# One decode step with a sliding key/value window on one core: how 512 output rows and two small inputs are loaded

## The chip, the cores and the metric

The kernel runs on one core of one Trainium2 chip. A core has four compute engines that run side by side, each with its own instruction stream: TensorE (PE, matrix products; its weight loads are listed as PEld), VectorE (DVE), ScalarE (ACT) and GpSimd (POOL). A fifth, SyncE (SP), here only issues transfers. Transfers between the main memory (HBM) and the on-chip memory (SBUF, 128 partitions) are carried out by 16 DMA engines, whoever issues them. The metric is the device time of one execution, in microseconds (us); lower is better.

## The reference

```python
xn = layernorm(x)                                   # x: 1 x 1 x 512
# A: attention over the last W = 4096 of 32768 cached positions, 32 heads of 128
q = xn @ wq                                         # 512 x 4096
p = softmax(q . k[window] / sqrt(128))              # per head
o = p @ v[window]
s = o.reshape(4096) @ wo                            # 4096 x 512
# B: a gated block of the same xn (for one token the shifted groups are all zero)
h  = gelu(layernorm(xn) @ w1); hs = shift(h) @ w2
x1 = xn + hs
g  = silu(x1 + gelu(layernorm(x1) @ w3) @ w4)       # w3: 512 x 1376
out = x + s * g
```

Everything is bfloat16. The window of K and of V is 32 heads x 4096 positions x 128, 33.5 MB each; wq and wo have 4.2 MB each, w2, w3 and w4 together 3.3 MB. Each element is used once or twice, so nearly all of the work is bringing it in.

## The kernel before

Loads go through one helper, which issues them from SP, in program order:

```python
def load(dst, src):
    return tc.keep_in_program_order(nc.sync.dma_start(out=dst, in_=src))

x_bf = small.tile([P, KC], BF16, name="x_bf")
nc.scalar.dma_start(out=x_bf[:], in_=A_x.rearrange("a b (p c) -> p (a b c)", p=P))
x_row = small.tile([P, P], BF16, name="x_row")
nc.gpsimd.memset(x_row[:], 0.0)
nc.scalar.dma_start(out=x_row[0:P:32, :], in_=A_x.rearrange("a b (j n) -> (a b j) n", j=KC))
w2_sb = ...; load(w2_sb[:], ...)                     # 512 KB
w3_sb = ...; load(w3_sb[:], ...)                     # 1376 KB
...                                                  # w4 in three parts, wq (4096 KB)
```

The layer norm of x, the block B and q come first. In the layer norm GpSimd computes the power -1/2:

```python
nc.gpsimd.tensor_tensor(out=rstd[:], in0=rstd[:], in1=neg_half[:], op=ALU.pow)
```

Then come 16 pairs of heads. K of a pair is one load of 2 MB over 128 partitions (six buffers), V another (three buffers, which take the space of the weights once q is there). DVE computes half of the scores of a pair (a product, line 302, and a sum, line 304), PE the other half through transposes; PE multiplies V:

```python
for s in range(NP + LAG):                            # NP = 16 pairs, LAG = 3
    h = s - LAG
    kn = load_kv(k_pool, A_k_cache, s) if s < NP else None
    if s == LAG:
        wts_guard.__exit__(None, None, None)         # the weights' space becomes V's
        v_pool = ctx.enter_context(tc.tile_pool(name="v", bufs=V_BUFS))
        wo_blk[few_block] = v_pool.tile([64, 8, D], BF16, tag="wo_few", bufs=1, name="wo_few")
        wo_rows = v_pool.tile([P, H - h_part, D], BF16, tag="wo_rows", bufs=1, name="wo_rows")
    if last:
        v = load_kv(v_pool, A_v_cache, h, cuts)      # the last V in three pieces
    elif h >= 0:
        v = load_kv(v_pool, A_v_cache, h)
    if h in (7, 12):
        load_wo(h // 12)
    if h == 4:
        load_few()
    if last:
        load_rows(H - 2, 2)
    ...
```

The output rows wo come in parts. Heads 0 to 15 and 16 to 23 are two blocks of 128 partitions (load_wo). Heads 28 to 31 (h_part = H - 4) are loaded row by row into wo_rows: heads 28 and 29 ahead of the last piece of V, heads 30 and 31 after it. Heads 24 to 27 are the part called wo_few, on 64 partitions with 8 rows (8 KB) each, loaded by GpSimd:

```python
def load_few():
    def step(k):
        nc.gpsimd.dma_start(out=scratch[0:k, :],
                            in_=A_x[0, 0, 0:4 * k].rearrange("(p c) -> p c", p=k))
    def part(p0, k):
        nc.gpsimd.dma_start(
            out=wo_blk[few_block][p0:p0 + 8 * k],
            in_=A_wo[few_h * P + 8 * p0:few_h * P + 8 * p0 + 64 * k, :].rearrange(
                "(a b t) n -> a b (t n)", a=k, b=8))
    scratch = small.tile([16, 4], BF16, name="scratch")
    step(15)
    part(0, 6)
    step(2)
    part(48, 2)
    step(7)
```

The step loads bring a few elements of x into a scratch tile that nothing reads[...]. In the built program GpSimd's order is: layer norm's power, step 15, step 2, the second layer norm's power, step 7, and then the two parts. All parts of wo are added into one PSUM tile, y_ps, by matmuls of one column of o (line 151). At the end y_ps is multiplied by g, x is added, and 1 KB is written out.

Of the kernel before, what the change touches and what calls it, by code (L numbers as in the profile page):

```python
# [8 lines left out]
P = 128  # L9
BF16 = mybir.dt.bfloat16  # L10
FP32 = mybir.dt.float32
# [7 lines left out]
G = 4  # L19
LAG = 3  # L20
K_BUFS = 6
V_BUFS = 3
EARLY = 4
LATE = 14
# [4 lines left out]
def kernel(  # L29
# [14 lines left out]
    nc = tc.nc  # L44
# [3 lines left out]
    _, H, Sk, Dh = A_k_cache.shape  # L48
# [6 lines left out]
    KC = D // P  # L55
# [13 lines left out]
    ps_o = ctx.enter_context(tc.tile_pool(name="ps_o", bufs=1, space=PSUM))  # L69
    ps_y = ctx.enter_context(tc.tile_pool(name="ps_y", bufs=1, space=PSUM))  # L70
    sm_pool = ctx.enter_context(tc.tile_pool(name="sm", bufs=3))
    small.tile([P, 128], BF16, name="pad")
    wts_guard = tc.tile_pool(name="wts", bufs=1)
    wts = wts_guard.__enter__()

    def load(dst, src):
        return tc.keep_in_program_order(nc.sync.dma_start(out=dst, in_=src))  # L77

    x_bf = small.tile([P, KC], BF16, name="x_bf")
    nc.scalar.dma_start(out=x_bf[:], in_=A_x.rearrange("a b (p c) -> p (a b c)", p=P))  # L80
    x_row = small.tile([P, P], BF16, name="x_row")
    nc.gpsimd.memset(x_row[:], 0.0)
    nc.scalar.dma_start(out=x_row[0:P:32, :], in_=A_x.rearrange("a b (j n) -> (a b j) n", j=KC))
    w2_sb = wts.tile([P, KC, D], BF16, name="w2_sb")
    load(w2_sb[:], B_w2.rearrange("(p c) n -> p c n", p=P))
    w3_sb = wts.tile([P, KC, F], BF16, name="w3_sb")
    load(w3_sb[:], B_w3.rearrange("(p c) n -> p c n", p=P))
    w4_sb = wts.tile([P, 11, D], BF16, name="w4_sb")
# [6 lines left out]
    def load_kv(pool, cache, i, cuts=None):  # L95
        t = pool.tile([P, CP, Dh], BF16, tag="kv", name="kv")
        src = cache[0, 2 * i:2 * i + 2, W0:, :].rearrange("a (b c) d -> b a (c d)", b=P // 2)
        dst = t[:].rearrange("p c d -> p (c d)")
        cuts = cuts or (0, CP)
        for c0, c1 in zip(cuts, cuts[1:]):  # L100
            load(dst[:, c0 * Dh:c1 * Dh], src[:, :, c0 * Dh:c1 * Dh])
            if len(cuts) > 2 and c1 == cuts[-2]:
                load_rows(H - 4, 2)
        return t

    ident_bf = const.tile([P, P], BF16, name="ident_bf")
# [41 lines left out]
    def rows_add(ps, col, w, last):  # L148
        k = col.shape[0]
        for j in range(KC):  # L150
            nc.tensor.matmul(ps[32 * j:32 * j + 1, :], lhsT=col, rhs=w[0:k, j * P:(j + 1) * P],
                             start=False, stop=last, skip_group_check=True)
# [102 lines left out]

    y_ps = ps_y.tile([P, P], FP32, name="y_ps")
    rows_open(y_ps)  # L260
# [83 lines left out]
    def sm_turn(g):  # L344

        s = st[g]
        mt_ps = ps_misc.tile([2, P], FP32, tag="misc", name="mt_ps")
        nc.tensor.transpose(mt_ps[:], s["m1"][:], ident_f[:])  # L348
        mx = sm_pool.tile([2, 2], FP32, tag="mx", name="mx")
        nc.vector.tensor_reduce(out=mx[:], in_=mt_ps[:].rearrange("r (b a) -> r a b", a=2), axis=AX.X,  # L350
                                op=ALU.max)
        nc.vector.scalar_tensor_tensor(out=md[0:2],  # L352
                                       in0=ident_f[0:2, 0:2].unsqueeze(2).to_broadcast([2, 2, 2]),
                                       scalar=-scale, in1=mx[:].unsqueeze(1).to_broadcast([2, 2, 2]),
                                       op0=ALU.mult, op1=ALU.mult)
# [27 lines left out]
    blocks = [(0, 16), (16, 8), (24, 8)]  # L383
    few_block = 2
    few_h = blocks[few_block][0]
    h_part = H - 4
    o_blk, wo_blk, ox_blk = {}, {}, {}

    def load_wo(i):
# [2 lines left out]
        wo_blk[i] = t[:, 0:n, :]  # L392
        load(wo_blk[i], A_wo[h0 * P:(h0 + n) * P, :].rearrange("(p t) n -> p t n", p=P))

    def load_few():
        def step(k):
            nc.gpsimd.dma_start(out=scratch[0:k, :],
                                in_=A_x[0, 0, 0:4 * k].rearrange("(p c) -> p c", p=k))  # L400

        def part(p0, k):
            nc.gpsimd.dma_start(
                out=wo_blk[few_block][p0:p0 + 8 * k],
                in_=A_wo[few_h * P + 8 * p0:few_h * P + 8 * p0 + 64 * k, :].rearrange(
                    "(a b t) n -> a b (t n)", a=k, b=8))

        scratch = small.tile([16, 4], BF16, name="scratch")
        step(15)
        part(0, 6)  # L410
        step(2)
        part(48, 2)
        step(7)

    def wo_row(h):
        return wo_rows[:, h - h_part, :]
# [1 line left out]
    def load_rows(h, n):  # L418
        load(wo_rows[:, h - h_part:h - h_part + n, :],
             A_wo[h * P:(h + n) * P, :].rearrange("(h p) n -> p h n", p=P))  # L420
# [32 lines left out]
    def v_out(h, n):  # L453
        g, hl = divmod(h, G)
        b = [i for i, (h0, _) in enumerate(blocks) if h >= h0][-1]
        if b not in o_blk:
            o_blk[b] = sm_pool.tile([P, blocks[b][1]], BF16, tag=f"o{b}", bufs=1, name="o")
            if b == few_block:
                nc.gpsimd.memset(o_blk[b][:], 0.0)
        c = h - blocks[b][0]  # L460
        if h >= h_part - 2:
            nc.vector.tensor_tensor(out=o_blk[b][:, c:c + n], in0=st[g]["oT"][:, hl:hl + n],  # L462
                                    in1=st[g]["rden"][:, hl:hl + n], op=ALU.mult)
            return
        for k in range(n):
            nc.scalar.mul(o_blk[b][:, c + k:c + k + 1], st[g]["oT"][:, hl + k:hl + k + 1],  # L466
                          st[g]["rden"][:, hl + k:hl + k + 1])
# [10 lines left out]
    def ox_pick(i):  # L478
# [10 lines left out]
                                    op=ALU.add)  # L489
        ox_blk[i] = ox  # L490


    y_row = small.tile([1, D], FP32, name="y_row")

# [7 lines left out]

    def y_block(i):
        for t in range(8):
            k = wo_blk[i].shape[0]
            rows_add(y_ps, ox_blk[i][0:k, t:t + 1], wo_blk[i][:, t, :], False)

    def y_head(h):
        rows_add(y_ps, o_blk[few_block][:, h - few_h:h - few_h + 1], wo_row(h), h == H - 1)
# [8 lines left out]
    for s in range(NP + LAG):  # L518
        h = s - LAG
        last = h == NP - 1  # L520
        kn = load_kv(k_pool, A_k_cache, s) if s < NP else None
        if s == LAG:
            wts_guard.__exit__(None, None, None)
            v_pool = ctx.enter_context(tc.tile_pool(name="v", bufs=V_BUFS))
            wo_blk[few_block] = v_pool.tile([64, 8, D], BF16, tag="wo_few", bufs=1, name="wo_few")
            wo_rows = v_pool.tile([P, H - h_part, D], BF16, tag="wo_rows", bufs=1, name="wo_rows")
        if last:
            v = load_kv(v_pool, A_v_cache, h, cuts)
        elif h >= 0:
            v = load_kv(v_pool, A_v_cache, h)  # L530
        if h in (7, 12):
            load_wo(h // 12)
        if h == 4:
            load_few()
        if last:
            load_rows(H - 2, 2)

        if s < NP:
            turn = [s // 2 - 1] if s % 2 == 0 and s > 0 else []
            k_open(s)  # L540
            k_vector(s, kn, 0)
            k_turn(s, kn)
            for g in turn:
                sm_turn(g)
            if s % 2 == 1 and s >= 3:
                sm_den((s - 3) // 2)
                sm_rden((s - 3) // 2)
            k_scores(s)
            if s % 2 == 1:
                sm_own(s // 2)  # L550
            for g in turn:
                sm_exp(g)
            if s in (12, 15):
                ox_spread(s // 14)
            if s == 11:
                v_add(3)
                v_out(12, 4)
            k_vector(s, kn, 1)
            if h >= 0:
                v_pair(h, v)  # L560
            if s in (12, 15):
                ox_pick(s // 14)
            if s == 13:
                y_wide(0)
            if s % 2 == 1:
                sm_max(s // 2)
            g = (h - 1) // 2
            if h > 0 and h % 2 == 1 and g not in MOVED:
                v_out(G * g, G)
            if h % 2 == 0 and h > 0 and g in MOVED and g != 3:  # L570
                v_add(g)
                v_out(G * g, G)
            if s == NP - 1:
                v_out(2 * h, 2)
        elif s == NP:

            sm_turn(LG)
            y_block(1)
            sm_exp(LG)
            rows_add(y_ps, one_f, y_row, False)  # L580
            v_pair(h, v)
            v_out(2 * h, 2)
            ox_spread(few_block)
            sm_den(LG)
            sm_rden(LG)
            ox_pick(few_block)
        elif not last:
            y_block(few_block)
            v_pair(h, v)
            v_out(2 * h, 2)  # L590
        else:
            for c0, c1 in zip(cuts, cuts[1:]):
                if c1 == CP:
                    for r in range(h_part, H - 2):
                        y_head(r)
                v_pair(h, v, c0, c1)
            v_out(2 * h, 2)
            for r in range(H - 2, H):
                y_head(r)
# [36 lines left out]
```

## Time and profile before

| | |
|---|---|
| time, median of 3 | 199.63 us (199.37 to 199.74) |
| span of the profiled execution | 197.8 us |
| read from HBM | 78.84 MB, 399 GB/s over the span |
| busy PE, PEld, DVE, ACT, POOL | 133.7, 103.2, 145.0, 78.9, 5.7 us |
| mean granted TensorE clock | 0.734 of full speed |

A row of 40 digits in the profile is the span in 40 equal slices of 4.94 us; a digit is the busy share in tenths, 9 for 90% or more. The row "DMA" is the mean share of the 16 DMA engines that have a packet in flight, and GB/s what they moved in the slice: the first can be full while the second is low. The chain of waits follows the work that ended last back from the end, at each step to what released it. In a group or a wait, "A <- B" says that A waited for B, and L302 is line 302 of the kernel.

### The profile page before, as it was taken

The page shows a single profiled execution, that of the slowest core. Times are in us where ns is not written, and L with a number is a line of the kernel's source. Part 1 is how long each engine was busy: PE and PEld are TensorE (multiplying, and loading weights), DVE is VectorE, ACT ScalarE, POOL GpSimd, SP SyncE. Part 2 cuts the span into 40 slices and gives each one's busy share as a digit, 9 for nine tenths or more (in the row PEclk, how much of TensorE's full clock was granted, in tenths as well). Part 3 has the DMA queues.
Part 4 walks back from the last instruction along what each step waited for, and adds up shares of the span by engine and source line. Part 5 has one row for each costly group of instructions (what it writes and reads, how often), then busy time and mean ns, then how long its engine had stood idle before and what let it go on. Part 6 is the DMA issues. An engine that isn't in the chain of part 4 may idle for free.

```text
span 197.8 us, 4706 instructions
## 1 busy us (share of the span) xinstructions
PE 133.7 (68%) x2099; PEld 103.2 (52%) x2099; DVE 145.0 (73%) x160; ACT 78.9 (40%) x173; POOL 5.7 (3%) x17
## 2 busy tenths in 40 slices
PE   0515976877478499759788862946575797875761
PEld 0415255866468393423788541336474636873660
DVE  1540012999999999999999999639899997792201
ACT  2000302978194391530676450335264308753000
POOL 2302100200000000000000000000000000000000
PEclk9999985696755855966967996698555879585555
DMA  6999999998999999999999999999999999999970
GB/s 200 410 444 451 388 424 421 406 257 335 427 426 437 437 426 421 424 434 427 434 427 431 427 421 427 437 427 434 424 427 431 431 424 431 421 437 424 406 279 6
DMA packets 6932, 79.13 MB, mean 400 GB/s; under 512 B 993, under 2 KB 1601, under 8 KB 2113
## 3 DMA queue, kind: packets, MB, share of 16 engines
q1 hardware_dynamic: 6568, 78.32, 95.0%
q0 software_dynamic: 192, 0.52, 1.0%
q8 instruction: 16, 0.26, 0.5%
q10 hardware_dynamic: 152, 0.00, 0.0%
q14 instruction: 4, 0.02, 0.0%
HBM read 78.84 MB, written 0.00 MB: 399 GB/s over the span
## 4 chain that ended last, share of the span: by engine, by line
DMA 44%; DVE 37%; PE 10%; ACT 2%; SPq 2%; issue 2%; POOL 1%; DVEq 0%
DMA kv<-in_A_k_cache_dram 31%; DVE S L304 22%; DVE prod L302 12%; DMA wo_rows<-in_A_wo_dram 7%; DMA scratch<-in_A_x_dram 4%; DMA x_bf<-in_A_x_dram 2%; ACT kt L318 2%; PE hr_ps L222 2%; PE qT_ps L238 2%; SPq L77 2%; PE oT L442 2%; PE a_ps L211 1%; PE hr_ps L219 1%; DVE m L342 1%; PE oT L449 1%
## 5 line engine op out<-in xcount | busy, mean ns | idle before, releaser
L304 DVE TENSOR_REDUCE S<-prod 128x20 f32<-128x2560 bf16 (+1 forms) x32 | 83.8, 2620 | 1.1
L318 ACT COPY kt<-pt 128x1024 bf16<-128x1024 bf16 x54 | 51.0, 1022 | 26.0 <-PE pt L317 26.0
L302 DVE TENSOR_TENSOR prod<-kv,q_bc 128x2560 bf16<-128x2560 bf16 (+1 forms) x32 | 44.3, 1386 | 8.9 <-DMA kv<-in_A_k_cache_dram 6.3
L317 PE MATMUL pt<-ident_bf,kv 128*128 128x128 bf16 x432 | 40.7, 276 | 10.6 <-DMA kv<-in_A_k_cache_dram 8.9
L317 PEld LDWEIGHTS <-kv 128*128 128x128 bf16 x432 | 37.0, 128 | 13.9 <-DMA kv<-in_A_k_cache_dram 10.4
L442 PE MATMUL oT<-pT,kv 128*128 128x2 bf16 x768 | 22.2, 165 | 3.6 <-DMA kv<-in_A_v_cache_dram 3.6
L323 PE MATMUL sT<-qT_bf,kt 128*128 128x2 bf16 x432 | 17.3, 165 | 10.8 <-ACT kt L318 10.2
L442 PEld LDWEIGHTS <-kv 128*128 128x128 bf16 x768 | 21.2, 102 | 5.0 <-DMA kv<-in_A_v_cache_dram 4.9
L323 PEld LDWEIGHTS <-kt 128*128 128x128 bf16 x432 | 15.8, 101 | 13.4 <-ACT kt L318 12.6
L431 PE MATMUL ov<-kv,pT 128*8 128x512 bf16 x64 | 20.5, 491 | 0.0
L431 PEld LDWEIGHTS <-pT 128*8 128x8 bf16 x64 | 6.4, 104 | 12.8 <-issue 9.4
L360 PE MATMUL mb_ps<-md,par_t 4*128 4x4 f32 x16 | 4.0, 315 | 12.0 <-DVE md L352 12.0
L367 ACT ACTIVATE pT<-S,mb 128x64 bf16<-128x64 f32 x32 | 10.9, 356 | 0.2
L363 ACT COPY mb<-mb_ps 128x4 f32<-128x4 f32 x8 | 1.3, 162 | 22.4 <-PE mb_ps L360 22.4
L360 PEld LDWEIGHTS mb_ps<-md,par_t 4*128 4x128 f32 x16 | 3.4, 264 | 12.6 <-issue 11.3
L462 DVE TENSOR_TENSOR o<-oT,rden 128x2 bf16<-128x2 f32 x3 | 0.5, 160 | 11.8 <-PE oT L442 11.8
L466 ACT ACTIVATE o<-oT,rden 128x1 bf16<-128x1 f32 x26 | 4.7, 264 | 5.7 <-PE oT L449 3.8
L225 DVE COPY hr<-hr_ps 1x512 f32<-1x512 f32 x1 | 0.7, 679 | 8.4 <-PE hr_ps L222 8.4
L214 ACT ACTIVATE a_bf<-a_ps 128x10 bf16<-128x10 f32 x1 | 0.2, 179 | 16.3 <-PE a_ps L211 16.3
L211 PE MATMUL a_ps<-z_bf,w_sb 128*128 128x1 bf16 (+1 forms) x44 | 2.6, 194 | 5.5 <-DVE z_bf L199 5.5
L367 ACT ACTIVATION_READ_ACCUMULATOR pT<-S,mb 128x1 f32 x32 | 6.0, 187 | 0.0
L348 PE MATMUL mt_ps<-ident_f,m 128*2 128x128 f32 x8 | 2.7, 340 | 4.5 <-DVE m L342 4.5
(111 smaller groups left out, 93.7 us busy)
## 6 DMA issues: line engine op xcount, KB each, us to landing
kv<-in_A_k_cache_dram SPq DMA_DIRECT2D x16, 2048.0 KB, 27.5
kv<-in_A_v_cache_dram SPq DMA_DIRECT2D x15, 2048.0 KB, 26.6
wq_sb<-in_A_wq_dram SPq DMA_DIRECT2D x1, 4096.0 KB, 18.6
wo<-in_A_wo_dram SPq DMA_DIRECT2D x1, 2048.0 KB, 27.0
w_sb<-in_B_w_dram SPq DMA_DIRECT2D x1, 1376.0 KB, 6.8
w_sb<-in_B_w_dram SPq DMA_DIRECT2D x1, 1024.0 KB, 8.9
wo<-in_A_wo_dram SPq DMA_DIRECT2D x1, 1024.0 KB
kv<-in_A_v_cache_dram SPq DMA_DIRECT2D x1, 1024.0 KB, 12.5
```

The lines of the kernel that those rows point to most:

```text
L77: return tc.keep_in_program_order(nc.sync.dma_start(out=dst, in_=src))
L211: nc.tensor.matmul(a_ps[0:m, j:j + 1], lhsT=w3_sb[:, c, cols], rhs=z3_bf[:, c:c + 1], start=(c == 0), stop=(c == KC - 1))
L302: nc.vector.tensor_tensor(out=prod[:, 0:m, :], in0=kn[:, rows, :], in1=q_bc[:, s:s + 1, :].to_broadcast([P, m, Dh]), op=ALU.mult)
L304: nc.vector.tensor_reduce(out=st[s // 2]["S"][:, s % 2, rows], in_=prod[:, 0:m, :], axis=AX.X, op=ALU.add)
L317: nc.tensor.transpose(pt[:, i, :], kn[:, n + b + i, :], ident_bf[:])
L318: nc.scalar.copy(out=kts[s][:, b:b + w, :], in_=pt[:, 0:w, :])
L323: nc.tensor.matmul(st[s // 2]["sT"][:, s % 2, c, :], lhsT=kt[:, c, :], rhs=qT_bf[:, 2 * s:2 * s + 2], start=True, stop=True)
L360: nc.tensor.matmul(mb_ps[:], lhsT=par_t[:].rearrange("k b a -> k (b a)"), rhs=md[:].rearrange("k r a -> k (r a)"), start=True, stop=True)
L367: nc.scalar.activation(out=s["pT"][:, i // 2, :, i % 2], in_=s["S"][:, i // 2, :], func=ACT.Exp, scale=scale, bias=mb[:, i:i + 1], accum_o ...
L431: nc.tensor.matmul(s["ov"][32 * r:32 * r + 8], lhsT=s["pT"][:, r, c:c + 4, :].rearrange("p i a -> p (i a)"), rhs=v[:, c:c + 4, :], start=F ...
L442: nc.tensor.matmul(s["oT"][:, 2 * r:2 * r + 2], lhsT=v[:, c, :], rhs=s["pT"][:, r, c, :], start=(c == 0), stop=(c == CP - 1))
L466: nc.scalar.mul(o_blk[b][:, c + k:c + k + 1], st[g]["oT"][:, hl + k:hl + k + 1], st[g]["rden"][:, hl + k:hl + k + 1])
```

## The change

The two small loads of x are issued by SP, behind w2, and no longer by ACT. The part wo_few becomes heads 24 and 25 only, on 32 partitions (two groups of 16, the other 32 partitions are zeros), loaded by SP in two loads, each with a source of 4 by 4 pieces of 8 rows; they stand after V of pair 11 and before K of pair 15. The step loads go. Heads 26 to 31 are loaded row by row. Since the rows of wo_few now lie on other partitions than before, a matmul with a small selecting matrix (few) brings the columns of o to them. What it is for: no transfers from GpSimd, and a choice of the DMA engines that carry wo_few.

```diff
+NE = 4
...
-    nc.scalar.dma_start(out=x_bf[:], in_=A_x.rearrange("a b (p c) -> p (a b c)", p=P))
     x_row = small.tile([P, P], BF16, name="x_row")
     nc.gpsimd.memset(x_row[:], 0.0)
-    nc.scalar.dma_start(out=x_row[0:P:32, :], in_=A_x.rearrange("a b (j n) -> (a b j) n", j=KC))
     w2_sb = wts.tile([P, KC, D], BF16, name="w2_sb")
     load(w2_sb[:], B_w2.rearrange("(p c) n -> p c n", p=P))
+    load(x_bf[:], A_x.rearrange("a b (p c) -> p (a b c)", p=P))
+    load(x_row[0:P:32, :], A_x.rearrange("a b (j n) -> (a b j) n", j=KC))
...
+    few = const.tile([P, 2, 32], BF16, name="few")
+    nc.vector.memset(few[:], 0.0)
+    for c in range(2):
+        nc.vector.tensor_copy(
+            out=few[:, c, 0:4 * NE].rearrange("p (a b) -> p a b", b=4),
+            in_=ident_bf[:, 4 * NE * c:4 * NE * (c + 1)].rearrange("p (b a) -> p a b", b=4))
...
-    h_part = H - 4
+    FEW = 8 * 8 * NE
+    h_part = few_h + FEW // P
...
     def load_few():
-        ... (step and part, as above)
+        t = wo_blk[few_block]
+        for c in range(2):
+            r0 = few_h * P + c * FEW // 2
+            load(t[32 * c:32 * c + 4 * NE],
+                 A_wo[r0:r0 + FEW // 2, :].rearrange("(b a t) n -> a b (t n)", b=4, a=NE))
...
+    def ox_few(i):
+        of_ps = ps_misc.tile([64, 8], FP32, tag="misc", name="of_ps")
+        nc.tensor.matmul(of_ps[:], lhsT=few[:].rearrange("p a b -> p (a b)"), rhs=ox_blk[i][:],
+                         start=True, stop=True)
+        of = sm_pool.tile([64, 8], BF16, tag="of", bufs=1, name="of")
+        nc.vector.tensor_copy(out=of[:], in_=of_ps[:])
+        ox_blk[i] = of
...
             wo_blk[few_block] = v_pool.tile([64, 8, D], BF16, tag="wo_few", bufs=1, name="wo_few")
+            nc.gpsimd.memset(wo_blk[few_block][:], 0.0)
...
         if last:
+            load_rows(h_part, 2)
             v = load_kv(v_pool, A_v_cache, h, cuts)
...
-        if h == 4:
+        if h == 11:
             load_few()
...
             sm_turn(LG)
+            ox_spread(few_block)
             y_block(1)
             sm_exp(LG)
+            ox_pick(few_block)
             rows_add(y_ps, one_f, y_row, False)
             v_pair(h, v)
             v_out(2 * h, 2)
-            ox_spread(few_block)
+            ox_few(few_block)
             sm_den(LG)
             sm_rden(LG)
-            ox_pick(few_block)
```

More of the change, by code (lines that the diff above doesn't have):

```diff
@@ L71 @@
     sm_pool = ctx.enter_context(tc.tile_pool(name="sm", bufs=3))
-    small.tile([P, 128], BF16, name="pad")
+    small.tile([P, 64], BF16, name="pad")
     wts_guard = tc.tile_pool(name="wts", bufs=1)
@@ L385 @@
     few_h = blocks[few_block][0]
-    h_part = H - 4
+    FEW = 8 * 8 * NE
+    h_part = few_h + FEW // P
+    assert FEW % P == 0 and h_part % 2 == 0
     o_blk, wo_blk, ox_blk = {}, {}, {}
@@ L397, in load_few @@
     def load_few():
[L398 to L413, printed above, removed]
+        t = wo_blk[few_block]
[3 more added lines that the diff above has]
+                 A_wo[r0:r0 + FEW // 2, :].rearrange("(b a t) n -> a b (t n)", b=4, a=NE))
     def wo_row(h):
@@ L460, in v_out @@
         c = h - blocks[b][0]
-        if h >= h_part - 2:
+        if h >= h_part:
             nc.vector.tensor_tensor(out=o_blk[b][:, c:c + n], in0=st[g]["oT"][:, hl:hl + n],
@@ L504, in y_block @@
         for t in range(8):
-            k = wo_blk[i].shape[0]
-            rows_add(y_ps, ox_blk[i][0:k, t:t + 1], wo_blk[i][:, t, :], False)
+            rows_add(y_ps, ox_blk[i][:, t:t + 1], wo_blk[i][:, t, :], False)
     def y_head(h):
```

## The prediction

> **What bounds the kernel now.** I read the page's second part first (the span in 40 slices), then its queue table, then the busy times by stretch of 2 us, then the chain of waits, and last the start on its own. From the page:
>
> ```profile
> DVE  1540012999999999999999999639899997792201
> DMA  6999999998999999999999999999999999999970
> GB/s 200 410 444 451 388 424 421 406 257 335 427 426 437 437 426 421 424 434 427 434 427 431 427 421 427 437 427 434 424 427 431 431 424 431 421 437 424 406 279 6
> q1 hardware_dynamic: 6568, 78.32, 95.0%
> q0 software_dynamic: 192, 0.52, 1.0%
> ```
>
> The DMA row is full from the second slice to the last but one, and the rate beside it stays near 428 GB/s: this kernel is a stream of 78.8 MB that never stops, and everything else fits beside it. Only two places fall short: the slices at 39.6 to 49.5 us (257 and 335 GB/s, though the engines count as busy), and the end. The same by stretches (us, then PE, PEld, DVE, ACT, POOL busy, granted clock, DMA share, GB/s):
>
> ```profile
> 22.00:38.00 16.00, 13.33 (x199) 9.90 (x197) 5.28 (x7) 4.71 (x8) 1.55 (x3) 0.68 1.02 429
> 38.00:46.00 8.00, 5.93 (x118) 5.38 (x117) 7.85 (x5) 6.40 (x9) 0.00 (x0) 0.93 1.02 268
> 48.00:168.00 120.00, 86.50 (x1230) 64.57 (x1231) 112.52 (x90) 54.78 (x124) 0.00 (x0) 0.73 1.01 428
> 186.00:190.00 4.00, 3.00 (x104) 2.63 (x97) 0.16 (x1) 0.00 (x0) 0.00 (x0) 0.50 0.98 391
> 190.00:194.00 4.00, 2.67 (x79) 1.97 (x75) 0.16 (x1) 0.00 (x0) 0.00 (x0) 0.50 0.40 148
> ```
>
> The dip has a DMA share of 1.02 at 268 GB/s: packets are in flight, but each takes longer. The packet records say the same: a 16 KB packet of the K stream takes 0.61 us before and after the dip and 1.06 us in it, on all engines. The 64 packets of 8 KB on the software queue run from 38.69 to 46.38 us, which is exactly the dip. They are the two GpSimd loads of wo_few:
>
> ```profile
> wo_few<-in_A_wo_dram POOLq DMA_DIRECT2D x1, 384.0 KB, 10.8
> wo_few<-in_A_wo_dram POOLq DMA_DIRECT2D x1, 128.0 KB, 11.9
> ```
>
> At the end the share is 0.40 for four microseconds: in the packet records sixteen transfers are in flight until about 189.5 us, then some nine until 192.5. Eight engines have finished and eight are still at it. The chain of waits, in order of time (start, us, what), closes on them:
>
> ```profile
> 8.43 7.09 DMA scratch<-in_A_x_dram
> 15.52 0.29 issue
> 15.81 0.54 POOL scratch L399
> ...
> 100.14 31.28 DMA kv<-in_A_k_cache_dram
> ...
> 139.42 30.91 DMA kv<-in_A_k_cache_dram
> ...
> 180.46 13.09 DMA wo_rows<-in_A_wo_dram
> 193.55 0.04 issue
> 193.59 0.41 PE y_ps L151 x8
> ```
>
> A load that needs 31 us from issue to landing stands in a queue some six loads deep, so the issuer is far ahead and only the engines' own rate counts. The scratch lines at the start are a wait in the front chain; I come back to them as a rival.
>
> [...]
>
> **The change part by part.**
> *The GpSimd load goes.* Lost in the dip: 8 us x (428 - 268) GB/s = 1280 KB, at 428 GB/s 2.99 us of the whole stream. Heads 24 to 27 were 512 KB in it; the bytes stay, since heads 24 and 25 come by the new load and heads 26 and 27 with the row loads, so nothing is to be added for them in the mean. Mean end of the engines: -2.99 us.
> *Skew of the old load.* Eight engines carried 64 KB more: 8 packets of 8 KB at 0.309 us (such packets of the V stream) = 2.47 us. The late half lies half of that over the mean: 1.24 us, which goes. The observed tail agrees: nine in flight for some 2.5 us.
> *Skew of the new load.* [...] 4 partitions of 8 KB each, twice, 64 KB per engine again. For c = 0 these are partitions 0 to 15, for c = 1 partitions 32 to 47[...]. [...] I expect packets of 0.31 us and no dip. But four engines are 2.47 us late, and the mean lies a quarter of that over the light ones, so the late ones stand 1.85 us over the mean: +1.85. It is queued between V of pair 11 and K of pair 15, and after it nothing gives the four their time back.
> *More rows in packets of 1 KB.* 256 KB more of wo_rows, 16 packets per engine, 0.046 us each instead of a sixteenth of a 0.61 us packet: +0.12 us.
> *x behind w2.* The two x loads take two issue slots of about 0.45 us ahead of w3. The w2 packets end near 4.0 us, and w3, issued at about 2.1 instead of 1.21 us, needs some 1.1 us to its first packet (w2: issued at 0.74, first packet at 1.80): 3.2 us, still in time. x itself lands up to 1 us later than 4.7 us. For the stream I take +0.1.
> *Small things off the path.* A GpSimd memset of wo_few, three little copies and one matmul, 8 more row matmuls (0.36 us) ahead of the last chunk of V, where PE waits for DMA anyway.
> Sum: -2.99 - 1.24 + 1.85 + 0.12 + 0.1 = -2.2 us. A second way, over the late engines alone: from the end of wq at 20.9 us, 240 packets of 16 KB (30 loads of 8 per engine) at 0.613 us, their mean in the steady stretch with instruction fetches in it, end at 168.0 us. The late engines stood at about 174.0 there (the last of the following wo packets end at 176.1 to 177.2, less 8 x 0.309), so they lost 6.0 us, their own 2.5 in it. After: -6.0 + 0.6 (more rows for all) + 2.5 = -2.9. Between the two I take -2.5: 199.6 - 2.5 = **197.1 us**.
>
> **The rivals.** *Front chain.* The second scratch load waits for the first, and GpSimd does the second layer norm's power only behind it, at 16.37 us though its input was there at 12.13: 4.2 us that disappear, so DVE starts K some 3 us earlier than 34.0. Were DVE the bound (it is full from 34 to 126 us), this would add 3 us, to about 194. Against it: DVE then idles (the 6 and 3 in its row), waiting for K, and the stream was full throughout. I count nothing. *The dip is not the load's doing*, but that of the first V loads into the space of the weights: then it stays, and only the skews change, -1.24 + 1.85 + 0.2, or 200.4. Against it: it begins at 38.6, with K packets still going, and ends with the software queue. *The new load spreads over all engines*: no skew at all, -4.0, or 195.6. *The four late engines hold up more than the end*: K of pair 15 lands late, V's buffers come free late, and light engines run dry before the last V pieces are issued. Now V of the last pair is issued at 177.25 us and starts near 183, so there are some 5 us to spare; it would have to cost over 2 us, for 199.5.
>
> **Range and chances.** The dip's gain is sure to some 0.6 us; the skew may be 0 or as computed; the rest is tenths. 8 in 10: 195.7 to 198.7. Over 2% faster means below 195.64, which asks for the spread load or the front chain as well: 0.09. Over 2% slower, above 203.6, needs a new stall of 4 us: 0.03. Within 2%: 0.88.
>
> **What would show it.** Right: no slice under 400 GB/s between the start and 185 us; the software queue gone from the table; a tail of about 2.5 us with four transfers in flight and some 100 GB/s; DVE's first product near 31 us with an end that doesn't follow it; the last landing near 191 instead of 193.5. Wrong: a dip that stays at 40 us without software packets; a new dip where wo_few loads (about 155 to 165 us); gaps in the DMA row before the end, which would mean that the issuer is late.

## The result and the profile after

The changed kernel takes 196.52 us (median of 6 runs, 196.01 to 197.66), the kernel before 199.58 (6 runs, 199.37 to 199.74): a ratio of 0.9855, with a 95% interval from 0.9827 to 0.9883. That is 3.1 us less; 197.1 us had been predicted. The total says little about the steps, though: some of them were right, and the errors of the others nearly cancelled, which was luck. The experiments are about telling these apart.

First the rows of the page that answer to those of before (40 slices of the span of 194.7 us), and its queues:

```profile
DVE  1650109999999999999999999089999986792001
DMA  5999999999999999999999999999999999999980
GB/s 149 392 449 431 411 424 424 429 421 431 431 428 431 428 426 424 431 431 431 424 431 424 428 428 431 431 431 428 428 431 428 431 422 433 424 434 423 409 313 8
q1 hardware_dynamic: 7032, 78.85, 96.0%
q8 instruction: 16, 0.26, 0.5%
```

The two slices of 257 and 335 GB/s are gone, and so is the software queue. New is a weaker start: 149 and 392 in the first two slices, where before had 200 and 410. The stretches of the trace after (us, length, then PE, PEld, DVE, ACT, POOL busy, granted clock, DMA share, GB/s):

```profile
4.00:6.00 2.00, 0.59 (x2) 0.50 (x2) 0.72 (x5) 0.00 (x0) 0.00 (x0) 1.00 0.74 253
...
38.00:46.00 8.00, 5.09 (x81) 4.76 (x81) 7.86 (x7) 5.27 (x7) 0.00 (x0) 0.79 1.02 431
48.00:168.00 120.00, 92.57 (x1261) 68.77 (x1262) 109.75 (x84) 56.12 (x135) 0.00 (x0) 0.66 1.01 429
186.00:188.00 2.00, 0.94 (x32) 0.93 (x32) 0.06 (x1) 0.00 (x0) 0.00 (x0) 0.50 0.86 337
188.00:190.00 2.00, 1.17 (x43) 1.02 (x40) 0.00 (x0) 0.00 (x0) 0.00 (x0) 0.50 0.60 219
190.00:192.00 2.00, 0.97 (x28) 0.44 (x16) 0.74 (x3) 0.00 (x0) 0.00 (x0) 0.50 0.03 10
```

Between 38 and 46 us the stream now runs at 431 GB/s at the same DMA share of 1.02; the steady part is unchanged (429). The tail isn't the one that was foretold: of sixteen transfers in flight some twelve are left from 187 to 189 us, and eight on average in the microsecond after it. A few engines finish early, where four were to finish late. The chain of waits after (start, us, what):

```profile
4.25 18.24 DMA wq_sb<-in_A_wq_dram
...
29.13 1.24 DVE prod L313
...
94.94 32.13 DMA kv<-in_A_k_cache_dram
...
137.41 29.53 DMA kv<-in_A_k_cache_dram
...
176.78 14.07 DMA wo_rows<-in_A_wo_dram
190.85 0.04 issue
190.89 0.41 PE y_ps L152 x7
```

DVE's first product starts at 29.13 us, 4.9 us earlier than before. That chain had:

```profile
34.02 1.24 DVE prod L302
```

The last landing comes only 2.7 us earlier: 190.85 against 193.55. The stream, not DVE, still ends the kernel. The packet records show wo_few as foreseen: four engines, 8 packets of 8 KB each, all of 0.309 us, between 157.3 and 161.6 us, and no dip beside them (the 16 KB packets stay at 0.611 us).

### The profile page after: what moved, and what is told of

Its sections match the earlier page's. It is cut to its first block, busy times and chain, and to the rows that moved or that the text cites. A ratio compares the mean times of both kernels' runs of the same rounds, so it can differ in the third digit from the quotient of the medians.

```text
span 194.7 us, 4727 instructions
## 1 busy us (share of the span) xinstructions
PE 138.0 (71%) x2108; PEld 106.3 (55%) x2108; DVE 145.3 (75%) x164; ACT 79.0 (41%) x173; POOL 6.3 (3%) x13
## 4 chain that ended last, share of the span: by engine, by line
DMA 48%; DVE 36%; PE 6%; SPq 3%; ACT 2%; issue 2%; POOL 1%; DVEq 0%; POOLq 0%
DMA kv<-in_A_k_cache_dram 32%; DVE S L315 22%; DVE prod L313 12%; DMA wq_sb<-in_A_wq_dram 9%; DMA wo_rows<-in_A_wo_dram 7%; SPq L78 3%; ACT kt L329 2%; PE oT L442 2%; PE qT_ps L239 2%; PE oT L449 1%; PE pt L328 1%; DVE m L353 0%; DVE S L349 0%; PE qb_ps L251 0%; ACT q_bc L253 0%
## 5 line engine op out<-in xcount | busy, mean ns | idle before, releaser
L328 PEld LDWEIGHTS <-kv 128*128 128x128 bf16 x432 | 37.5, 129 | 13.4 <-DMA kv<-in_A_k_cache_dram 9.8
L442 PEld LDWEIGHTS <-kv 128*128 128x128 bf16 x768 | 21.6, 103 | 5.5 <-DMA kv<-in_A_v_cache_dram 5.5
L431 PE MATMUL ov<-kv,pT 128*8 128x512 bf16 x64 | 21.4, 509 | 0.0
L507 PE MATMUL yr_ps<-wo,ox 128*1 128x512 bf16 x16 | 6.2, 574 | 0.0
L157 PE MATMUL ln_ps<-x_f,ones_f 128*128 128x4 f32 x4 | 1.2, 365 | 5.8 <-DVE x_f L180 4.7
```

The lines of the kernel that those rows point to most:

```text
L328: nc.tensor.transpose(pt[:, i, :], kn[:, n + b + i, :], ident_bf[:])
L431: nc.tensor.matmul(s["ov"][32 * r:32 * r + 8], lhsT=s["pT"][:, r, c:c + 4, :].rearrange("p i a -> p (i a)"), rhs=v[:, c:c + 4, :], start=F ...
L442: nc.tensor.matmul(s["oT"][:, 2 * r:2 * r + 2], lhsT=v[:, c, :], rhs=s["pT"][:, r, c, :], start=(c == 0), stop=(c == CP - 1))
L507: nc.tensor.matmul(yr_ps[:], lhsT=ox_blk[i][:, t:t + 1], rhs=wo_blk[i][:, t, :], start=(t == 0), stop=(t == n - 1))
```

## The experiments

**What slows the stream: where the bytes land, or who issues them?** Before's dip had been laid to wo_few's place on partitions 0 to 63, an assumption of the author's that no run had shown. Moving it to the upper half, still from GpSimd, should decide. Against the kernel before:

```diff
-                out=wo_blk[few_block][p0:p0 + 8 * k],
+                out=wo_blk[few_block][64 + p0:64 + p0 + 8 * k],
...
-            wo_blk[few_block] = v_pool.tile([64, 8, D], BF16, ...)
+            wo_blk[few_block] = v_pool.tile([P, 8, D], BF16, ...)
```

> The kernel before, with the two GpSimd loads of wo_few writing partitions 64 to 127 in place of 0 to 63 (the matmuls use those partitions; they multiply them with the columns that belong to other heads, so the output differs, but every load and every matmul is there in the same size). Same queue, same engines, same bytes, same time of issue. [...] the dip at 38 to 46 us is gone or small, and eight engines end 2.5 us late: about 196.2. Rival 'software queue' (whatever GpSimd issues slows the stream): the dip stays at some 268 GB/s and the time at 199.6.

Measured: 199.59 us, ratio to before 1.0024 (1.0013 to 1.0035). The dip stays. The same stretches in its trace:

```profile
22.00:38.00 16.00, 13.69 (x206) 10.18 (x205) 5.55 (x7) 4.99 (x8) 1.05 (x2) 0.71 1.01 426
38.00:46.00 8.00, 6.62 (x116) 6.19 (x114) 7.83 (x6) 6.00 (x8) 0.00 (x0) 0.73 1.04 283
```

283 GB/s against 268. So the lower half is not special: written to the upper half, the load does the same. The run decides less than it was made for, though. It took for granted that eight engines carry the load, and the trace of the kernel before says otherwise. In the full stream an engine starts its next packet some 4 ns before the last one ends, so its packets can be followed one after the other. Of the sixteen chains found in this way each has four of the software queue's 64 packets of 8 KB: all sixteen engines carried wo_few. Both runs have it on one half of the partitions, so where the bytes land isn't ruled out. Next the other side, GpSimd's queue. wo_few goes back to partitions 0 to 63, but as one load from SP, without the step loads. Against before:

```diff
-        (step loads and the two GpSimd parts)
+        load(wo_blk[few_block][:],
+             A_wo[few_h * P:few_h * P + 512, :].rearrange("(p t) n -> p (t n)", p=64))
```

> The kernel before, with wo_few (same 512 KB, same partitions 0 to 63, same place behind V of pair 4's issue in program order) as one load from SP in place of the scratch loads and the two loads from GpSimd. [...] a dip shows where it moves, some 2 to 3 us long in engine time: 196.5 to 198. Rival 'software queue': no dip, 32 KB more per engine and nothing else: about 194.9.

Measured: 199.49 us, ratio 1.0018 (1.0007 to 1.0029). There is no software queue any more, 38 to 46 us runs at 426 GB/s, and the dip has moved to where SP's queue reaches this load:

```profile
82.00:84.00 2.00, 1.97 (x6) 0.97 (x7) 1.97 (x2) 1.34 (x8) 0.00 (x0) 0.50 0.97 414
84.00:86.00 2.00, 2.00 (x8) 0.69 (x7) 2.00 (x1) 0.25 (x2) 0.00 (x0) 0.72 1.22 295
86.00:88.00 2.00, 2.00 (x19) 1.05 (x18) 1.93 (x3) 0.55 (x2) 0.00 (x0) 1.00 0.90 201
88.00:90.00 2.00, 1.40 (x27) 1.23 (x25) 2.00 (x1) 2.00 (x4) 0.00 (x0) 1.00 0.96 270
90.00:92.00 2.00, 1.44 (x52) 1.35 (x53) 2.00 (x3) 1.14 (x2) 0.00 (x0) 0.99 0.98 418
```

At 428 GB/s as the norm, the three low stretches lose 2 us x (133 + 227 + 158) = 1036 KB, or 2.4 us. GpSimd's queue isn't needed for a dip. (Its time also holds another effect, found below.) What is left is where the bytes land, and that was tried last, with everything else kept. Against the changed kernel, the same source pieces and number of engines, to partitions 64 to 79 and 96 to 111 in place of 0 to 15 and 32 to 47. The matmuls of heads 24 and 25 then read zeros, so their share of the output is left out:

```diff
-            load(t[32 * c:32 * c + 4 * NE],
+            load(t[64 + 32 * c:64 + 32 * c + 4 * NE],
...
-            rows_add(y_ps, ox_blk[i][:, t:t + 1], wo_blk[i][:, t, :], False)
+            k = ox_blk[i].shape[0]
+            rows_add(y_ps, ox_blk[i][:, t:t + 1], wo_blk[i][0:k, t, :], False)
...
-            wo_blk[few_block] = v_pool.tile([64, 8, D], BF16, ...)
+            wo_blk[few_block] = v_pool.tile([P, 8, D], BF16, ...)
```

> The changed kernel, with the two wo_few loads writing partitions 64 to 79 and 96 to 111 in place of 0 to 15 and 32 to 47 (the matmuls read the zeros in 0 to 63, so heads 24 and 25 are missing from the output; loads and matmuls are all there). Same queue, same source, [...] same bytes. [...] a dip at 155 to 162 us, like that of the 64-partition load from SP, which lost 2.4 us[...]: 198 to 199. Rival 'number of engines or source' (the dip comes of reading 8 KB pieces of wo by more than four engines): no dip, 196.5.

Measured: 199.44 us, ratio 1.0012 (0.9992 to 1.0032): the whole gain of the change is gone. The stretches around the load:

```profile
154.00:156.00 2.00, 2.00 (x6) 0.50 (x4) 2.00 (x2) 0.00 (x0) 0.00 (x0) 0.50 1.03 434
156.00:158.00 2.00, 2.00 (x6) 0.63 (x5) 1.89 (x5) 0.00 (x0) 0.00 (x0) 0.50 1.16 414
158.00:160.00 2.00, 2.00 (x15) 0.86 (x13) 2.00 (x1) 0.35 (x1) 0.00 (x0) 0.85 0.97 201
160.00:162.00 2.00, 1.79 (x36) 1.66 (x33) 0.10 (x1) 2.00 (x3) 0.00 (x0) 1.00 1.02 217
162.00:164.00 2.00, 0.86 (x23) 0.60 (x19) 1.92 (x4) 1.96 (x3) 0.00 (x0) 1.00 0.90 324
164.00:166.00 2.00, 1.99 (x64) 1.95 (x65) 1.93 (x1) 1.25 (x8) 0.00 (x0) 0.85 1.04 442
```

The loss is 2 us x (227 + 211 + 104) = 1084 KB or 2.5 us, from 256 KB on four engines. The packet records between 158 and 162.5 us show both kinds doubled: 8 KB packets have a median of 0.627 us (0.309 in the changed kernel), and 16 KB packets of the K stream 1.25 us (0.611), none of them under 0.89. So the destination partitions alone make this dip, and GpSimd has no part in it. All twelve engines that carry nothing of wo_few have packets of over 1.2 us as well. The traces don't show which engine writes which partitions, and why the twelve are slowed stays open.

**What does wo_few cost in all?** Against before, nothing in place of the loads; the output rows of heads 24 to 27 are left out (zeros):

```diff
-        (step loads and the two GpSimd parts)
+        nc.gpsimd.memset(wo_blk[few_block][:], 0.0)
```

> The kernel before, with the loads of wo_few and the scratch loads left out (the rows of heads 24 to 27 are zeros, so their part of the output is missing): what they cost in all. 512 KB in an even stream are 1.2 us. [...] the late engines as counted in the prediction (6.0 us lost): 193.7. If the dip is given back later (buffers, compute): 197 or more.

Measured: 196.14 us, ratio 0.9853 (0.9838 to 0.9868), and no dip (422 GB/s from 38 to 46 us). That is less than the dip and the 512 KB together. Something else had become slower, and the next run showed it too.

**The front chain.** The changed kernel with the three step loads put back, for nothing but their delay of GpSimd:

```diff
     def load_few():
+        def step(k): ...                 # as in the kernel before
+        scratch = small.tile([16, 4], BF16, name="scratch")
+        step(15)
+        step(2)
+        step(7)
         t = wo_blk[few_block]
```

> The changed kernel, with the three small scratch loads from GpSimd put back (and with them the wait of the second layer norm's power for the first of them), but not the wo_few loads from GpSimd. Theory 'stream' (only the DMA stream's own rate counts): DVE starts some 4 us later, near 33 us, and the time stays at 196.5 within 0.4. Rival 'front chain' (the 3 us came from DVE starting at 29.1 instead of 34.0): 199 to 200.

Measured: 198.3 us, ratio 0.996 (0.9944 to 0.9976): most of the gain lost, which would speak for the front chain. But the loss isn't at the start. The packet records have a mean of 614.7 ns for a 16 KB packet between 62 and 94 us (the few over 700 ns left out), against 611.2 in the kernel before and the changed kernel, and that is long after DVE has caught up. The kernels whose packets take 614.7 to 614.9 ns are those in which the experiment added or took away a small tile (scratch, or the one that ox_few fills): in the built programs the tiles of the weights, and V's after them, then begin 32 bytes beyond a multiple of 64 (K's stay where they were). In the kernel before and the changed one V's begin at a multiple of 256; the change had made the padding tile smaller too, 64 elements instead of 128. The shift is an unintended second change in five kernels: this one, the one without wo_few, the one with wo_few from SP, and two that follow. So the same kernel was run once more with a padding tile 32 bytes smaller, which puts those tiles back:

```diff
-    small.tile([P, 64], BF16, name="pad")
+    small.tile([P, 48], BF16, name="pad")
```

> The first scratch experiment again, with the padding tile 32 bytes smaller, because the scratch tile had pushed the weights and V tiles from a multiple of 256 bytes to 32 bytes past one, and the 16 KB packets of that run took 614.7 ns on average instead of 611.2. The two kernels differ in that one size. Theory 'stream' with 'alignment' (3.5 ns on some 300 packets per engine is 1.0 us): back to 611 ns, and 196.5 to 197.2 although DVE starts 4 us later. Rival 'front chain': stays at 198.3 or more.

Measured: 196.71 us, ratio 0.9869 (0.9848 to 0.989), the changed kernel's time within the intervals; packets are back at a mean of 611.3 ns. The pair in the steady stretch (columns as above), first the trace of the shifted kernel, then that of the aligned one:

```profile
48.00:168.00 120.00, 88.14 (x1287) 67.01 (x1288) 114.01 (x91) 57.11 (x137) 0.00 (x0) 0.68 1.01 426
```

```profile
48.00:168.00 120.00, 90.73 (x1301) 68.17 (x1302) 115.27 (x92) 57.56 (x137) 0.00 (x0) 0.67 1.01 429
```

And in the aligned one's chain of waits (start, us, what) the front is as long as before the change:

```profile
7.96 7.84 DMA scratch<-in_A_x_dram
...
34.00 1.24 DVE prod L313
```

DVE starts at 34.0 us instead of 29.1 and the time doesn't follow: the front chain's 3 us aren't there, and the intervals leave room for 1 us at most. The run without wo_few was aligned in the same way (padding of 144 elements in place of 128):

```diff
-    small.tile([P, 128], BF16, name="pad")
+    small.tile([P, 144], BF16, name="pad")
```

> The kernel before without the loads of wo_few and of scratch (heads 24 to 27 missing from the output), with 32 bytes more of padding, aligned as the kernel before. Alignment theory: 1.0 us less than the unaligned one (196.1), so 195.1. Then the load of wo_few cost 4.3 us in all, of which 1.2 us are its bytes and 3.0 the dip, and its engines carried no skew: the eight late engines of the prediction would make it 193.7. Some five engines should be as late as before against the first ones, by 3.3 us.

Measured: 194.62 us, ratio 0.9767 (0.9745 to 0.9788). So the loads of wo_few, with the step loads, cost the kernel before 2.3% (2.1 to 2.6), 4.6 us. Its 512 KB at 428 GB/s are 1.2 of them and the dip 3.0; 0.4 is left over, which is as large as the interval.

**The skew.** The prediction let eight engines carry wo_few before and four after, all of them late at the end. To see what four engines cost, heads 24 and 25 were loaded row by row as well, in 1 KB packets on all engines, with everything else as in the changed kernel:

```diff
-    h_part = few_h + FEW // P
+    h_part = few_h
...
         if h == 11:
-            load_few()
+            load_rows(h_part, 2)
...
-            y_block(few_block)
+            for r in range(h_part, h_part + 2):
+                y_head(r)
```

> The changed kernel, with heads 24 and 25 loaded row by row over all 16 engines at the same place in the queue, in place of the two loads over four engines; no wo_few, its matmuls replaced by those of two heads, the output is the reference's. The prediction's step: four engines are 1.85 us later than the mean, so without them 194.7. Theory 'slack' (other engines end late for another reason, the instruction fetches, and the four had room): the last end moves by 0.3 to 0.8 only, 195.9.

Measured: 199.01 us, ratio 0.9985 (0.9974 to 0.9996): slower than the changed kernel, but with packets of 614.7 ns, so the shift is in it. The same with x on ACT's queue, as before the change:

```diff
+    nc.scalar.dma_start(out=x_bf[:], in_=A_x.rearrange(...))
...
+    nc.scalar.dma_start(out=x_row[0:P:32, :], in_=A_x.rearrange(...))
...
-    load(x_bf[:], A_x.rearrange(...))
-    load(x_row[0:P:32, :], A_x.rearrange(...))
```

> Both edits on the changed kernel: x on ACT's queue, and heads 24 and 25 row by row. If the two add up: 194.0 with the prediction's skew, 195.2 with the theory 'slack' and the bubble.

Measured: 197.81 us, ratio 0.9924 (0.9908 to 0.994), packets of 614.9 ns. And the last kernel aligned by the padding:

```diff
-    small.tile([P, 64], BF16, name="pad")
+    small.tile([P, 80], BF16, name="pad")
```

> The changed kernel with x on ACT's queue and heads 24 and 25 row by row, with 32 bytes more of padding, so that the V tiles start at a multiple of 256 bytes as in the changed kernel. Alignment: 1.0 us less than without the padding, 196.8. Against the changed kernel with x on ACT's queue alone (195.45): the prediction's skew says 1.85 less, 193.6; theory 'slack' (the last engines are late from instruction fetches, and now carry 16 KB more each) says 0.6 to 0.9 more, 196.2.

Measured: 196.19 us, ratio 0.985 (0.9826 to 0.9875), packets of 611.1 ns. Against its twin that keeps wo_few on four engines (the next run, 195.45), rows on all engines cost about 0.7 us more, though the intervals overlap a little. With the prediction's skew they would have saved 1.85. The reason lies in the packet records, in the times at which the sixteen engines begin the last block of wo (aligned runs; us):

```
before               171.2-171.5 (6 engines)  172.0-173.0 (5)  174.2-174.7 (5)
heads 24-31 by rows 166.9-167.3 (6)          167.7-168.9 (5)  170.1-170.3 (5)
```

The second row is the kernel just told (heads 24 and 25 by rows, x on ACT), and its engines stand 3.3 us apart with no wo_few at all. The aligned kernel without any wo_few shows the same: 166.3-166.6 (6), 167.1-168.1 (5), 169.6-169.8 (5). The spread comes from something else: 16 instruction fetches of 16 KB (queue q8), each of 0.93 to 1.13 us. At a fetch, the starts of one engine's stream packets stand 1.66 and 1.1 us apart instead of twice 0.61, so that engine loses 1.55 us. The trace doesn't name the engines, but each of them closes its share of a load with a packet of 4 bytes, sixteen per load, and from load to load these show who falls back. In the kernel before, one engine goes from 0.31 to 1.86 us behind the first at the fetch of 60.7 us, another from 1.94 to 3.49 at that of 114.8 us, and the others keep their distances. By the block of wo thirteen of the sixteen fetches have begun, and two of 8 KB (57.5 and 73.4 us), which cost an engine some 1.0 us each. Six engines with none, five with one and five with two make these fifteen, and they are the three groups of the first row. In the changed kernel, the four engines of wo_few reach it at 157.3 to 159.2 us; without their 2.47 us each they would begin the wo block at 167.0 to 168.9 us, among the early ones. With it they begin at 169.5 to 171.4, the others' latest at 170.8. The load fills mostly time that these engines had to spare. The last microseconds agree: with rows on all engines 8 or 9 transfers are in flight from 187 to 189 us, and in the twin with wo_few on four engines 12 or 13 from 185.5 to 188 us. Some four more engines work to the end.

**The two loads of x.** The changed kernel with only x back on ACT's queue:

```diff
+    nc.scalar.dma_start(out=x_bf[:], in_=A_x.rearrange(...))
...
+    nc.scalar.dma_start(out=x_row[0:P:32, :], in_=A_x.rearrange(...))
...
-    load(x_bf[:], A_x.rearrange(...))
-    load(x_row[0:P:32, :], A_x.rearrange(...))
```

> The changed kernel, with the two loads of x on ACT's queue again. Prediction's term: +0.1 for x behind w2, so 196.4. Theory 'bubble' (in the changed kernel's trace the stream moves 253 GB/s at 4 to 6 us against 410 before, 0.7 us of the stream): 195.8, and the rate at 4 to 6 us back at 400.

Measured: 195.45 us, ratio 0.9816 (0.9792 to 0.9841), the fastest version here that computes everything. The other way round, the kernel before with x from SP behind w2:

```diff
-    nc.scalar.dma_start(out=x_bf[:], in_=A_x.rearrange(...))
...
-    nc.scalar.dma_start(out=x_row[0:P:32, :], in_=A_x.rearrange(...))
...
+    load(x_bf[:], A_x.rearrange(...))
+    load(x_row[0:P:32, :], A_x.rearrange(...))
```

> The kernel before, with this part of the change alone: the two loads of x from SP behind w2. Prediction's term: 199.7. Theory 'bubble': 200.3, and 253 GB/s at 4 to 6 us.

Measured: 200.35 us, ratio 1.0041 (1.0022 to 1.006). Both agree on some 0.8 us. It can be seen from 4 to 6 us. With x from SP it is 253 GB/s in the changed kernel (above) and 270 in this run; with x from ACT it is 410 before and 396 in the changed kernel. The stretch in three traces, one line each (columns as above): before, before with x from SP, the changed kernel with x on ACT.

```profile
4.00:6.00 2.00, 0.59 (x2) 0.50 (x2) 0.50 (x4) 0.00 (x0) 0.00 (x0) 1.00 1.03 410
```

```profile
4.00:6.00 2.00, 0.64 (x3) 0.56 (x3) 0.88 (x5) 0.00 (x0) 0.00 (x0) 1.00 0.83 270
```

```profile
4.00:6.00 2.00, 0.59 (x2) 0.50 (x2) 0.69 (x4) 0.00 (x0) 0.00 (x0) 1.00 0.98 396
```

In the changed kernel the transfers in flight fall to between 6 and 9 from 3.75 to 4.5 us: the engines' last w2 packets end from 3.65 to 3.96 us, and w3's first sixteen start from 3.87 to 4.82 us. Before, these start from 3.85 to 4.22 us, just as w2's end (3.90 to 4.20). 157 GB/s less for 2 us is 0.73 us of the stream.

## Why the prediction held, step by step

- **What bounds the kernel: right.** The stream sets the end. DVE's start moved by 4.9 us; put back to 34.0 us (step loads, aligned) the time stays within the intervals.
- **The dip, -2.99: right.** With the load gone the stretch is at 431 GB/s. The cause that the author had assumed, eight engines writing to partitions 0 to 63, was half right. A load from SP dips too (201 GB/s at 86 to 88 us), and in the changed kernel the place alone makes one: 64 partitions further up, its load takes the rate to 201 and 217 GB/s. But the writers weren't eight engines: all sixteen took part. And with only four engines writing elsewhere the packets of all sixteen double (0.611 to 1.25 us), which the assumption doesn't explain.
- **"Skew of the old load", -1.24: wrong.** Eight engines with 64 KB more don't exist: all sixteen carried four packets each. Behind the load the thirteen engines without a fetch stand within 0.39 us of each other, as they did ahead of it (fifteen within 0.37). The engines that begin the wo block late in the kernel before are those with most instruction fetches, and without any wo_few the tail is there as well: 8 to 11 transfers in flight from 185 to 187.5 us. The step that failed is how many engines carry the load: eight was an assumption of the author's, which the tail only seemed to confirm. Nothing of the skew went. The "own 2.5" of the late engines in the second way is the same mistake; what holds them 3 us behind the first are two fetches each.
- **"Skew of the new load", +1.85: wrong.** The four engines, which the prediction only assumed, and their 2.47 us are there, but "nothing gives the four their time back" overlooked that they had time over against the engines with more fetches. The end sees little of these 256 KB: the last of the four begins the wo block 0.6 us behind the latest other engine in the profiled run, not 2.47. If it saw nothing, the term would be -0.61 by the prediction's count from the mean (256 KB at 428 GB/s) instead of +1.85.
- **1 KB rows, +0.12: fits, but isn't shown by itself.** With the slack, heads 24 and 25 by rows should cost 0.61 + 0.12 = 0.73 us more than on four engines; about 0.7 was measured for the two together, give or take as much.
- **x behind w2, +0.1: mis-sized.** About 0.8 us. The two slots took 0.41 and 0.71 us instead of 0.45 each, so that w3 was issued at 2.40 us and not at 2.1, and its first packet came 1.5 us later, not 1.1. So w3 wasn't "still in time": at 3.87 us, most of w2's packets had run out.

With the sizes found (-0.61 if the end sees nothing of the new load, 0.12 as predicted): -2.99 + 0 - 0.61 + 0.12 + 0.8 = -2.7 us; measured -3.1, with an interval from -3.5 to -2.3. The prediction's -2.2 and -2.9 came near by luck, since the two wrong skews (-1.24 and +1.85, together +0.61) and the small x term missed in opposite directions. Of the rivals, the front chain and a dip from other loads are refuted, and so is a new load spread over all engines (it ran on four), though the end behaves almost as that rival said, for another reason. Nor did the four engines hold up anything before the end: from 10 us on the rate stays at 409 or more up to the slice that ends at 185 us.

## What to carry to other kernels

In a kernel that is one long stream, look for the places where the DMA share is full and the rate is not, and for the ends of the single engines. Here 256 KB on four engines with time to spare cost some 0.7 us less than on all sixteen, though the intervals of the two runs touch. For a load to fewer than 128 partitions, try more than one place among the partitions and look at the packets of the stream around it: here the same 256 KB cost 3 us more on partitions 64 to 79 and 96 to 111 (199.44 us) than on 0 to 15 and 32 to 47 (196.52). And when an experiment adds or removes a tile, look at the mean packet of an untouched stretch first: a shift of the other tiles can be larger than the effect in question.

## What was not expected of the hardware

- With V's tiles 32 bytes past a multiple of 64, the 16 KB packets of K and V take 614.7 to 614.9 ns on average instead of 611.1 to 611.3. Three pairs that differ in the padding alone, each run measured against the kernel before, give 0.9% (0.996 and 0.9869), 0.7% (0.9924 and 0.985) and 0.9% (0.9853 and 0.9767), 1.5 to 1.8 us. The packets explain some 0.9 us of it (256 packets of K, V and wo per engine x 3.5 ns); the rest wasn't traced.
- At the two followed in the kernel before (60.7 and 114.8 us), an instruction fetch of 16 KB costs its engine 1.55 us of the stream, more than the 0.93 to 1.13 us of a fetch itself. The fetches fall unevenly, none to two on an engine, and leave the engines 3.3 us apart when they reach the last block of wo.
- A load of 256 KB on four engines, written 64 partitions further up, takes the rate of the whole stream from 428 to 201 and 217 GB/s for four microseconds and to 324 for two more, and slows the packets of all engines. Why those of the others are slowed was not found out.
